# K and V loaded two heads at a time, on alternate partitions: a two-layer decode step on one Trainium2 core

## The chip, the core and the metric

The kernel runs on one core of one Trainium2 chip. A core has five engines that run their own instruction streams and meet at semaphores: TensorE (PE, with its weight loads shown apart as PEld), VectorE (DVE), ScalarE (ACT), GpSimd (POOL) and SyncE (SP), which here only issues DMAs. Data comes from HBM through 16 DMA engines into SBUF, which has 128 partitions; TensorE writes its products to PSUM, which has eight banks (here six tensors `bank0` to `bank5` and one tensor `pair` that holds the other two). The metric is the device time of one execution in microseconds (us).

## The reference

Eight batch rows of width 448 go through attention, an MLP, the same attention again and the same MLP again, each with a residual; layer norms have no weights.

```
x = x + A(layernorm(x));  x = x + B(layernorm(x));  x = x + A(layernorm(x));  x = x + B(layernorm(x))

A(x): q = (x @ wq) as [8 rows, 16 heads, 256]
      k, v = the last 1024 of 4096 positions of the caches [8 rows, 8 kv heads, 4096, 256]
      each kv head serves 2 of the 16 q heads
      o = softmax(q . k / 16) @ v;   return o (4096 wide) @ wo [4096, 448]
B(x): return silu(x @ w1 [448, 1792]) @ w2 [1792, 448]
```

Everything is bf16. Both layers use the same caches, so 64 pairs of a K head and a V head are read, each array 1024 x 256 x 2 bytes = 512 KB and contiguous in HBM; the next head of the same row begins 4096 x 256 x 2 bytes = 2 MiB further on. That is 67.1 MB of the 78.2 MB that the kernel moves.

## The kernel before

**Slots and loads.** A K or V head is one DMA of 512 KB (`load_kv`, L496): partition p gets eight consecutive positions, 4 KB in one piece. There are R = 30 slots of 4 KB per partition. The loads go round the slots in the order row 0 K heads 0 to 7, row 0 V heads 0 to 7, row 1 K, and so on (`seq`, `pump`), all on SP's queue, after `wq` (three loads with 8 KB per partition, L438), with `w2`, `wo` and `w1` in between. A load waits on SP until every reader of the load 30 places earlier is done. As a row takes 16 loads, V heads 6 and 7 of row b wait for K heads 0 and 1 of row b-1, K heads 0 to 5 of row b+1 for K heads 2 to 7 of row b-1, and K heads 6, 7 of row b+1 and V heads 0 to 5 of row b+1 for V heads 0 to 7 of row b-1. Whatever stands behind a waiting load on SP waits too.

**One row.** K is transposed in place by VectorE in blocks of 32 x 32 four-byte words (`transposes`, L639), four heads in one instruction each (128x1024 words) and four in two (128x512). `scores` (L656) multiplies block-diagonal queries (`qbd`) with the transposed K, four heads of a half k2 at a time on four column tiles of TensorE. `softmax` takes the maximum (L673), spreads it over groups of partitions (`mq` L674, matmul `mx` with `quad` L675, `mb` L677), takes the exponential (L688), permutes it with one matmul (`perm`, L690), transposes it on VectorE (`turn`, L692), sums it (`l`, L694) and inverts the sum (L697). `products` (L703) and `products_late` (L712, heads 6 and 7 of layer 1 and all of the last row's layer 2) multiply with V. `o_turn` (L725 to L733) turns the result, `wo_rows` (L754) multiplies with `wo`, `fold` (L760, L529, L532) adds the residual. `chain` is the MLP of layer 1 and the queries of layer 2: `stats` (L771 to L776), `w1_half` (L544, L549), tanh and product (`up`, L798 to L806), `w2` (L818), `wq` (L833, L838), `qm` and `qx` (L839, L846, L850).

**Order.** Row b's chain and its second attention (`attend2`, `values2`) are interleaved with the transposes, scores and products of row b+1 (`attend1`, `values1`); K and V of a row stay in their slots until layer 2 has read them. The order on PE, DVE, ACT and POOL is written out as task numbers in `ORDER`; each engine runs its list strictly in that order, and `Plan.emit` puts semaphore waits between tasks that share keys. The durations given with the tasks don't enter the program. SP's list is the program's order.

**The end.** The output projection and MLP of layer 2 are made for rows 0 to 6 together (`final_rows`, scratch in a slot of row 6), and for row 7 alone (`final_last`). `final_rows` begins with ten small VectorE instructions for the constants `fold8` and `f8a` (L874, L878, L880). In `up` for the last row, `th` (L801) multiplies with `rhalf` before `hT` (L803).

## Time and profile before

| | us |
|---|---|
| three timed runs: median (lowest to highest) | 231.98 (231.31 to 232.46) |
| the profiled execution: its own time | 230.15 |
| the profiled execution: its span, first to last instruction | 228.4 |
| busy: PE / DVE / ACT / POOL | 173.0 / 157.2 / 71.4 / 22.8 |

The granted TensorE clock is 1.00 throughout. The page divides the span into 40 slices of 5.7 us; a digit 9 is 90% busy or more. A group of instructions is told by its line, engine and operation, then written tile <- read tiles, shapes, count, busy time and the mean of one in ns. A matmul's duration is from its start to its modelled end, and matmuls overlap, so the time of a whole run of them in the chain or the timeline is the better price.

### The profile page before, as it was taken

To read this page: it belongs to the slowest core of one execution; us is meant where nothing else is said; L and a number is where in the kernel's file an instruction comes from. 1 tells how busy PE (TensorE), PEld (TensorE's weight loads), DVE (VectorE), ACT (ScalarE), POOL (GpSimd) and SP (SyncE) were. 2 spreads that over 40 slices of the span, in tenths; PEclk is the share of its full clock that TensorE was granted. 3 is DMA by queue.
4 is the path that set the end of the run, shared out by engine and by line. 5 is a ranking of instruction groups with operands and counts; after the bars stand their busy time and mean duration, and the time that the engine had idled before them with its cause. 6 is when DMAs were issued, how large, how long until landed. Compare 5 with 4: busy or idle time off the path is not lost.

```text
span 228.4 us, 8452 instructions
## 1 busy us (share of the span) xinstructions
PE 173.0 (76%) x3779; PEld 94.1 (41%) x3779; DVE 157.2 (69%) x369; ACT 71.4 (31%) x218; POOL 22.8 (10%) x41
## 2 busy tenths in 40 slices
PE   0020737357878989999898987888989999999894
PEld 0010623123444455445444644554445445544662
DVE  6238989878792797389459837974895589314644
ACT  2000080633302341432324142414332431353341
POOL 1000130000200210101010101110120200000020
PEclk9999999999999999999999999999999999999999
DMA  6999999999999999999999999999999999700000
GB/s 175 413 406 407 382 380 395 411 414 417 405 400 369 377 408 403 396 408 407 406 406 408 402 378 411 408 392 395 410 409 385 380 408 406 307 3 3 0 6 1
DMA packets 22681, 78.21 MB, mean 342 GB/s; under 512 B 2279, under 2 KB 5302, under 8 KB 22262
## 3 DMA queue, kind: packets, MB, share of 16 engines
q1 hardware_dynamic: 22486, 77.32, 86.6%
q8 instruction: 29, 0.48, 0.9%
q10 hardware_dynamic: 160, 0.36, 0.6%
q14 instruction: 6, 0.05, 0.1%
HBM read 77.67 MB, written 0.01 MB: 340 GB/s over the span
## 4 chain that ended last, share of the span: by engine, by line
PE 46%; DVE 31%; DMA 10%; ACT 6%; issue 4%; SPq 2%; DVEq 0%; ACTq 0%
DVE slot L639 12%; DMA slot<-in_A_k_cache_dram 10%; PE bank L656 10%; PE bank L703 7%; DVE slot L472 7%; PE pair L754 6%; PE bank L781 2%; PE pair L833 2%; ACT ot L760 2%; PE bank L675 2%; PE bank L846 2%; PE bank L712 2%; PE bank L833 2%; PE pair L529 2%; PE pair L818 1%
## 5 line engine op out<-in xcount | busy, mean ns | idle before, releaser
L639 DVE STREAM_TRANSPOSE slot<-slot 128x512 uint32<-128x512 uint32 (+1 forms) x96 | 80.2, 866 | 7.0 <-DMA slot<-in_A_k_cache_dram 6.8
L656 PE MATMUL bank<-slot,qbd 128*16 128x256 bf16 (+1 forms) x1024 | 40.9, 285 | 5.1 <-DVE slot L639 2.0
L703 PE MATMUL bank<-slot,qbd 128*24 128x512 bf16 (+6 forms) x416 | 31.1, 393 | 3.5 <-DVE qbd L692 3.3
L656 PEld LDWEIGHTS bank<-slot,qbd 128*16 128x16 bf16 (+1 forms) x1024 | 23.2, 87 | 16.7 <-ACT qbd L850 4.0
L781 PE MATMUL bank<-wq_sb,cols 128*1 128x512 bf16 x192 | 19.6, 416 | 13.9 <-DMA wq_sb<-in_A_wq_dram 13.9
L776 POOL TENSOR_TENSOR fcols<-fcols 128x1 f32<-128x1 f32 x17 | 9.4, 554 | 106.4 <-ACT fcols L774 94.5
L754 PE MATMUL pair<-wo_sb,q1s 128*1 128x449 bf16 x288 | 17.2, 353 | 1.1 <-DVE wo_sb L475 0.8
L850 ACT ACTIVATE qbd<-bank 128x256 bf16<-128x256 f32 x16 | 6.1, 384 | 33.5 <-PE bank L846 33.5
L725 ACT ACTIVATE ot<-bank,q1s 128x512 bf16<-128x512 f32 (+1 forms) x16 | 10.8, 673 | 16.4 <-PE bank L703 11.1
L626 POOL TENSOR_TENSOR qbd<-q1s,fcols 128x256 bf16<-128x256 bf16 x16 | 9.7, 614 | 59.7 <-PE bank L712 42.4
L703 PEld LDWEIGHTS bank<-slot,qbd 128*24 128x24 bf16 (+6 forms) x416 | 9.7, 92 | 11.1 <-DVE qbd L692 4.2
L692 DVE STREAM_TRANSPOSE qbd<-bank 128x256 bf16<-128x256 bf16 x17 | 8.0, 473 | 8.2 <-PE bank L690 7.9
L673 DVE TENSOR_REDUCE q1s<-bank 128x1 f32<-128x256 f32 x15 | 6.3, 423 | 8.1 <-PE bank L656 8.0
L472 DVE TENSOR_REDUCE slot<-wo_sb 128x6 f32<-128x2688 bf16 x4 | 11.8, 2948 | 0.1
L781 PEld LDWEIGHTS bank<-wq_sb,cols 128*1 128x1 bf16 x192 | 4.2, 82 | 15.4 <-issue 13.9
L674 ACT ACTIVATE q1s<-fcols,q1s 128x4 f32<-128x4 f32 x15 | 4.4, 296 | 18.7 <-DVE q1s L673 18.7
L675 PE MATMUL bank<-q1s,quad 128*128 128x4 f32 x30 | 6.0, 269 | 4.7 <-ACT q1s L674 4.5
L598 PE MATMUL pair<-slot,wq_sb 128*128 128x16 bf16 x128 | 3.6, 174 | 7.5 <-DVE slot L591 7.5
L833 PE MATMUL pair<-wq_sb,q1s 128*1 128x256 bf16 x256 | 8.9, 275 | 0.3 <-DVE q1s L765 0.3
L688 ACT ACTIVATE qbd<-bank,q1s 128x256 bf16<-128x256 f32 x15 | 7.1, 472 | 6.3 <-DVE q1s L677 6.0
L712 PE MATMUL bank<-slot,qbd 128*7 128x256 bf16 (+7 forms) x192 | 8.6, 283 | 0.6 <-DVE qbd L692 0.6
L833 PE MATMUL bank<-wq_sb,q1s 128*1 128x512 bf16 x128 | 8.8, 390 | 0.0
(168 smaller groups left out, 244.6 us busy)
## 6 DMA issues: line engine op xcount, KB each, us to landing
slot<-in_A_k_cache_dram SPq DMA_DIRECT2D x64, 512.0 KB, 8.3
slot<-in_A_v_cache_dram SPq DMA_DIRECT2D x64, 512.0 KB, 10.1
wo_sb<-in_A_wo_dram SPq DMA_DIRECT2D x4, 896.0 KB, 14.6
wq_sb<-in_A_wq_dram SPq DMA_DIRECT2D x3, 1024.0 KB, 8.0
w_sb<-in_B_w_dram SPq DMA_DIRECT2D x1, 1568.0 KB, 19.8
w_sb<-in_B_w_dram SPq DMA_DIRECT2D x1, 1344.0 KB, 17.2
wq_sb<-in_A_wq_dram ACTq DMA_DIRECT2D x1, 256.0 KB, 3.5
wq_sb<-in_A_wq_dram SPq DMA_DIRECT2D x1, 256.0 KB, 4.1
```

The source lines that it names most:

```text
L472: dve(lambda e, rows=rows, s=s: e.tensor_reduce(s, rows[:, :, R0:M1].rearrange("p c (a n) -> p c a n", a=2), AX.X, ALU.add, negate=True), ...
L626: pool(lambda e, k2=k2: e.tensor_tensor(qdata(0, k2), q1s[:, b, 64 * k2:64 * k2 + 64].rearrange("p (n r) -> p n r", r=2).unsqueeze(3) .bro ...
L639: dve(lambda e, v=v: e.transpose(v, v), keys, keys, 0.15 + n / 2 / 950, b, ("KW%d" if n > 1024 else "KT%d") % k)
L656: fns.append(lambda e, w=w, j=j, kv=kv, cb=cb, par=par: e.matmul(sc[32 * j:32 * j + up_to, 0:256], w, kv, start=(cb == 0 and par == 0), st ...
L675: pe(lambda e: e.matmul(mx, quad[:], mq, start=True, stop=True, skip_group_check=True), [K[4], "quad"], bk(LB[n]), 0.2, b, "mx%d" % L)
L703: pe([lambda e, t=t: e.matmul(bank[ob][32 * t:32 * t + m, :], pT_sb[L][:, 64 * t:64 * t + m], v[:, 512 * t:512 * t + 512], start=True, sto ...
L712: pe([lambda e, t=t, a=a: e.matmul(o[32 * t:32 * t + m, :], pT_sb[n][:, 64 * t + a:64 * t + a + m], v[:, 512 * t + DH * a:512 * t + DH * a ...
L725: act(lambda e: e.activation(o_t, src[1], ACTF.Copy, scale=sm[b][:, 4 * L + 3:4 * L + 4]), bk(src[0]) + [("sm", b, L, 3)], okey, 0.62, b, ...
L754: fns.append(lambda e, i=i, w=w, c0=c0: e.matmul(bank[XB][32 * (i % 4):32 * (i % 4) + 1, c0:c0 + D + 1], oT[:, oT_col(i):oT_col(i) + 1], w ...
L776: pool(lambda e: e.tensor_tensor(rhalf, var4, nhalf, ALU.pow), ["var4", "nhalf"], ["rhalf"], 0.54, b, "pow" + name)
L781: pe([lambda e, i=i: e.matmul(bank[OB[0]][32 * i:32 * i + 1, :], zero_b, wq_sb[:, 512 * i:512 * i + 512], start=True, stop=True, tile_posi ...
L833: pe([lambda e, j=j, c=c, qh=qh, k2=k2, h=h, n=n: e.matmul(qh[32 * j:32 * j + 1, :], xbt[b][:, xcol(c, k2):xcol(c, k2) + 1], view(wq_sb[:] ...
```

## The change

K and V heads are loaded in pairs. A slot is 8 KB per partition and there are 15 of them. Partition 2i + e of a pair gets sixteen consecutive positions of head e, 8 KB in one piece, so the two heads lie on alternate partitions. One DMA moves 1 MB. Only the very last pair (row 7, V heads 6 and 7) comes in two DMAs, each the first or second half of all rows, 4 KB per partition. The transposes now write each 32 x 32 block with the sixteen columns of the even partitions ahead of the sixteen of the odd ones, so that the scores' moving operand can pick a head. A product with V covers both heads of a pair: each `products` task is one half of a pair (the first or second 4 KB of each partition), with the other head's rows made zero. The softmax's permutation becomes four matmuls of 128 columns, with shifted views of two tables, and writes every other word; `mx` becomes four matmuls with 32-column weights; `mq` has 16 columns and one buffer. For the last row the factor `rhalf` moves behind the `w2` product, with the residual evicted apart by ScalarE (`resL`). The constants `fold8` and `f8a` are made behind row 1's second attention (`fold_consts`). The orders of the four engines are new.

```diff
-    R = 30
-    WIDE = (0, 1, 2, 3)
+    R = 15
+    NP = HKV // 2
+    WIDE = (0, 1)
+    SLOT = 4096
...
-    def load_kv(s, cache, b, kvh):
+    def load_kv(s, cache, b, j, apart):
         extra = SCRATCH[s] if s in SCRATCH and s not in first_use else []
         first_use.add(s)
-        dma(lambda e: e.dma_start(slots[s][:, :].rearrange("p (u d) -> p u d", d=DH),
-                                  cache[b, kvh, S0:SK, :].rearrange("(p u) d -> p u d", p=P)),
-            slot_key(s) + extra, W * DH * 2, "slot%d" % s)
+        a = cache[b, 2 * j, S0:SK, :]
+        step = SLOT // 2 if apart else SLOT
+        for h in range(SLOT // step):
+            src = bass.AP(a.tensor, a.offset + h * step, [[SLOT, 64], [SK * DH, 2], [1, step]])
+            dma(lambda e, h=h, src=src: e.dma_start(slots[s][:, h * step:(h + 1) * step], src),
+                slot_key(s, h if apart else None) + extra, P * step * 2, "last%d" % h if apart else "slot%d" % s,
+                rate=407e3 if apart else 417.7e3)
...
-    def transposes(b, k):
-        s = slot_of[b, "k", k]
-        n = 2048 if k in WIDE else 1024
-        for h in range(2048 // n):
-            v = slots[s][:, h * n:(h + 1) * n].bitcast(U32)
-            keys = slot_key(s) if n > 1024 else [("slot", s, h)]
-            dve(lambda e, v=v: e.transpose(v, v), keys, keys, 0.15 + n / 2 / 950, b,
-                ("KW%d" if n > 1024 else "KT%d") % k)
+    def transposes(b, j):
+
+        s = slot_of[b, "k", j]
+        for h in range(2):
+            for i0, i1 in ((0, 2),) if j in WIDE else ((0, 1), (1, 2)):
+                v = slots[s][:, 2048 * h + 1024 * i0:2048 * h + 1024 * i1].bitcast(U32)
+                keys = [("slot", s, 2 * h + i) for i in range(i0, i1)]
+                dve(lambda e, v=v, i0=i0, i1=i1: e.transpose(view(v, 0, [(32, 16 * (i1 - i0)), (1, 16), (16, 2)]), v), keys, keys,
+                    0.15 + (i1 - i0) * 512 / 950, b, ("KW%d" if i1 - i0 > 1 else "KT%d") % (2 * j + h))
...
-                    kv = slots[slot_of[b, "k", 4 * k2 + j]][:, :].rearrange(
-                        "p (u cb jj par) -> p cb par u jj", u=8, cb=4, par=2)[:, cb, par, :, :]
+                    kv = view(slots[slot_of[b, "k", 2 * k2 + j // 2]][:, :], 64 * cb + 32 * (j % 2) + par, [(256, 16), (2, 16)])
...
-            act(lambda e: e.activation(mq, sel4, ACTF.Copy, scale=mneg), [K[0], "sel4"], [K[4]], 0.2, b, "mq%d" % L)
-            pe(lambda e: e.matmul(mx, quad[:], mq, start=True, stop=True, skip_group_check=True), [K[4], "quad"],
-               bk(LB[n]), 0.2, b, "mx%d" % L)
+            act(lambda e: e.activation(mq, sel16, ACTF.Copy, scale=mneg), [K[0], "sel16"], ["mq"], 0.2, b, "mq%d" % L)
+            pe([lambda e, t=t: e.matmul(mx[32 * t:32 * t + 32, :], quad[:], mq[:, 4 * t:4 * t + 4], start=True, stop=True,
+                                        tile_position=(0, 32 * t), skip_group_check=True) for t in range(4)],
+               ["mq", "quad"], bk(LB[n]), 0.06, b, "mx%d" % L)
...
-        pe(lambda e: e.matmul(px, perm[:], e_sb[m], start=True, stop=True),
+        pe([lambda e, h=h, u=u: e.matmul(px[:, h:256:2], perm[h][:, 16 - 16 * u:144 - 16 * u],
+                                         e_sb[m][:, 128 * u:128 * u + 128], start=(u == 0), stop=(u == 1),
+                                         skip_group_check=True) for h in range(2) for u in range(2)],
            EK[m] + PERM + QM * m, bk(LB[n]), 0.13, b, "perm%d" % L)
...
-    def products(b, L, kvh, ob):
-        v = slots[slot_of[b, "v", kvh]]
-        m = 4 * (HKV - kvh)
-        pe([lambda e, t=t: e.matmul(bank[ob][32 * t:32 * t + m, :], pT_sb[L][:, 64 * t:64 * t + m],
-                                    v[:, 512 * t:512 * t + 512], start=True, stop=True, tile_position=(0, 32 * t),
-                                    skip_group_check=True) for t in range(4)],
-           slot_key(slot_of[b, "v", kvh]) + PT[L], bk(ob), 0.055, b, "PV%d" % L)
+    def products(b, L, j, ob):
+        v = slots[slot_of[b, "v", j]]
+        m = 8 * (NP - j)
+        for h in range(2):
+            pe([lambda e, t=t, h=h: e.matmul(
+                bank[ob][32 * t:32 * t + m, :], pT_sb[L][:, 64 * t + 32 * h:64 * t + 32 * h + m],
+                v[:, 2048 * h + 512 * t:2048 * h + 512 * t + 512], start=(h == 0), stop=(h == 1),
+                tile_position=(0, 32 * t), skip_group_check=True) for t in range(4)],
+               slot_key(slot_of[b, "v", j], h) + PT[L], bk(ob), 0.055, b, "PV%d" % L)
...
-            if name == "L":
-                dve(lambda e, t=t: e.tensor_scalar(t, t, 1.0, rhalf, op0=ALU.add, op1=ALU.mult), [("th", h), "rhalf"],
-                    [("th", h)], 0.12, b, "th" + n)
...
+    def fold_consts(n, row):
+        SM0 = [("sm", 0, L, i) for L in range(2) for i in range(5)]
+        for x in range(4):
+            dve(lambda e, x=x: e.tensor_copy(fold8[32 * x:32 * x + 32, :], ident[32 * x:32 * x + 32, 32 * x:32 * x + n]),
+                ["ident"], [("fold8", x)] + SM0, 0.08, row, "f8a")
+        for a in range(2):
+            dve(lambda e, a=a: e.tensor_copy(f8a[a], fold8), FOLD8 + SM0, [("f8a", a)], 0.08, row, "f8a")
+            for x in (1 - a, 3 - a):
+                dve(lambda e, a=a, x=x: e.memset(f8a[a][32 * x:32 * x + 32, :], 0.0), [("f8a", a)],
+                    [("f8b", a, x)], 0.08, row, "f8a")
...
-        dve(lambda e: e.tensor_copy(orow, ob[:, 0:T]), bk(OB[1]) + KEY, ["orowL"], 0.18, b, "orowL")
+        dve(lambda e: e.scalar_tensor_tensor(out=orow, in0=ob[:, 0:T], scalar=rhalf, in1=res, op0=ALU.mult, op1=ALU.add),
+            bk(OB[1]) + ["rhalf", "resL"] + KEY, ["orowL"], 0.2, b, "orowL")
...
-    seq = [(b, t, k) for b in range(NB) for t in "kv" for k in range(8)]
+    seq = [(b, t, k) for b in range(NB) for t in "kv" for k in range(NP)]
...
-    cap = [R - 2]
+    cap = [R - 1]
...
-        for kvh in range(HKV - LATE):
-            products(b, 0, kvh, OB[0])
+        for j in range(NP - 1):
+            products(b, 0, j, OB[0])
...
+        if b == 1:
+            fold_consts(NBF, 2)
```

## The prediction, written before the result was known

> **What bounds the kernel now.** I read the slices first, then the DMA rate by windows, then who waits for whom on SP and VectorE, then the groups by form, then the timeline of VectorE at the start and at the end. The slices of the page:

> ```profile
> DMA  6999999999999999999999999999999999700000
> GB/s 175 413 406 407 382 380 395 411 414 417 405 400 369 377 408 403 396 408 407 406 406 408 402 378 411 408 392 395 410 409 385 380 408 406 307 3 3 0 6 1
> ```

> The DMA engines are full from slice 2 to slice 34, that is to about 199 us, and then nothing is left to load: 28 us of computing on the last row follow. So the end is the end of the loads plus a tail. The loads run at 380 to 417 GB/s. The windows (start:end, length, then PE, PEld, DVE, ACT, POOL, clock, DMA share, GB/s) show what the rate depends on:

> ```profile
> 8.00:12.00 4.00, 0.00 (x0) 0.00 (x0) 0.00 (x0) 0.00 (x0) 0.00 (x0) 1.00 1.01 422
> 40.00:44.00 4.00, 1.54 (x10) 0.60 (x10) 3.30 (x7) 2.18 (x9) 0.00 (x0) 1.00 1.03 410
> 60.00:64.00 4.00, 3.41 (x81) 1.76 (x79) 2.89 (x7) 1.00 (x3) 0.55 (x1) 1.00 1.03 410
> 68.00:72.00 4.00, 3.24 (x74) 1.64 (x67) 1.09 (x5) 1.25 (x4) 0.00 (x0) 1.00 1.00 358
> 172.00:176.00 4.00, 3.56 (x87) 2.18 (x80) 1.79 (x5) 1.13 (x4) 0.00 (x0) 1.00 1.01 379
> ```

> From 8 to 12 us `wq` arrives in pieces of 8 KB: 422 GB/s. From 40 and from 60 V and K arrive in pieces of 4 KB: 410. The trace's packet records say the same: 4096 bytes take 160 ns (median; mean 165.5), 8192 bytes 314 (median). The dips to 358 and 379 fall behind moments when SP had been held by a slot. The waits, of SP and of VectorE (total, times, longest):

> ```profile
> SPq L496 <- PE bank L656: 59.5, 12, 8.9
> SPq L496 <- PE bank L703: 26.6, 18, 4.0
> DVE slot L639 <- DMA slot<-in_A_k_cache_dram: 6.8, 9, 1.8
> ```

> SP waits long, yet the DMA engines stay full, because loads are queued. Counting bytes issued less bytes landed, the queue is lowest when the second scores release K heads 0 and 1: 0.7 to 1.1 MB at 66.9, 88.7, 108.6, 130.1, 151.6, 172.6 and 193.1 us. That is 1.8 us of cover at 410 GB/s, and the period is 21.0 us per row. VectorE in turn waits for K, 5.6 of the 6.8 us between 60 and 161 us, and not once after 161. So loads and computing run in step, loads slightly ahead as the bound until 161 us.

> The instructions that the change touches (groups by form):

> ```profile
> L639 DVE STREAM_TRANSPOSE slot<-slot 128x512 uint32<-128x512 uint32 x64 | 41.2, 683 | 0.7 <-DMA slot<-in_A_k_cache_dram 0.7
> L639 DVE STREAM_TRANSPOSE slot<-slot 128x1024 uint32<-128x1024 uint32 x32 | 39.2, 1234 | 6.3 <-DMA slot<-in_A_k_cache_dram 6.1
> L692 DVE STREAM_TRANSPOSE qbd<-bank 128x256 bf16<-128x256 bf16 x17 | 8.0, 473 | 8.2 <-PE bank L690 7.9
> L690 PE MATMUL bank<-qbd,perm 128*128 128x256 bf16 x17 | 4.9, 289 | 3.1 <-ACT qbd L688 2.9
> ```

> **The change, part by part.**

> *Loads in 8 KB pieces.* 67.1 MB at 410 GB/s are 163.7 us, at 422 159.0: 4.7 us less. By the medians (2 x 160 against 314 ns) it is 1.9%, 3.1 us; by the mean of all 4 KB packets (331 against 314) 5.2%, 8.5 us, which would also cure the dips. The 422 was measured while no engine worked, so I stay between the first two: 4.0 us. Of the bytes, 39 of 187 us' worth come after 161 us, when nobody waited for them, so 79% pass on: **-3.2 us** (0 to -8.5). SP issues 65 loads in place of 128; an issue is 0.43 us against 1.28 us of transfer and never was the limit.

> *Pairs as the unit.* The first head of a pair is usable 1.28 us later (512 KB at 410). A load now waits for both heads of the pair it replaces, and all later loads stand behind it on SP, but K heads are already released four at a time by the scores, so only releases by V products get coarser. At the start the first transpose (15.8 us) moves to about 17.1; VectorE then has 0.6 us of waits for K and small idle gaps to give: **+0.3 us** (0 to 1.3). In steady state the lateness comes off the 1.8 us of cover, at nothing; without the cover it is 1.28 us in each of six rows (rival 3).

> *Transposes.* Same count and shapes, but the output alternates between two places 64 bytes apart. L692 also writes in a permuted pattern (steps of 4 bytes): 473 ns for 256 columns, against 445 for the plain one of L549 on 256 columns. Timeline of VectorE at the start:

> ```profile
> 6.03 0.35 DVE L403 TENSOR_REDUCE slot<-ident 128x32 f32<-128x128 bf16 x1
> 7.23 0.29 DVE L407 TENSOR_REDUCE slot<-ident 128x32 f32<-128x128 bf16 x1
> 29.36 1.28 DVE L604 TENSOR_TENSOR slot<-slot 128x256 bf16<-128x256 f32 x1
> ```

> L407 reads 128 elements in a row, L403 the same 128 in steps of 64 bytes: 0.06 us more, about 0.5 ns each. L604 writes 256 two-byte results in steps of 64 bytes and takes 1.28 us, where L591 (40 elements, 0.193) and L566 (8, 0.16) lead to 0.42: 3.4 ns more for each. I take **0**, from L692, because it is the nearest in kind (the same operation, with an output that is permuted inside a block), and because here each 16 bytes are filled within eight successive writes; the ends are 0 (the count of columns is the same, so no gain) and 3.4 ns per column over 65,536 columns, rival 1. [...]

> *Softmax.* `perm`: one matmul (0.28 us) becomes four of 128 columns; four of 64 columns (L846) span 0.42 in the chain, so about 0.53, +0.25 us. `mx`: two passes with 128-column weights (0.39) become eight with 32-column weights; the eight of L694 span 0.24, -0.15 us. In all +0.1 us in each of 15 softmaxes; in steady state TensorE's work lies beside loads that set the pace (cover as above; uncovered 1.5 us in all). In the tail one `perm` of row 7's layer 2 and the last layer 1 softmax are on the path: **+0.4 us**. Products and scores keep their number and columns; weights of 32 in place of 28 columns cost 399 against 396 ns: nothing.

> *The tail.* In row 7 the constants sit between steps of the chain:

> ```profile
> 204.98 0.47 DVE L549 STREAM_TRANSPOSE pair<-pair 128x256 f32<-128x256 f32 x1 [0.90 <-PE pair L544]
> 205.47 0.16 DVE L874 COPY slot<-ident 32x7 bf16<-32x7 bf16 x1
> 205.60 0.40 DVE L549 STREAM_TRANSPOSE bank<-bank 128x192 f32<-128x192 f32 x1
> 206.03 0.17 DVE L874 COPY slot<-ident 32x7 bf16<-32x7 bf16 x1
> 206.23 0.16 DVE L806 SCALAR_TENSOR_TENSOR q1s<-q1s,pair 128x8 bf16<-128x8 f32 x1
> ```

> From the first transpose to L806 it is 1.25 us here, 0.83 in the row before (164.98 to 165.81): -0.4. At 209.73 to 210.97 (L838 to L839) the memsets of L880 cost another 0.4 (1.24 against 0.84). Leaving out `th` (L801) saves 0.2 at 224.4. Together **-1.0 us**. The ten small instructions go to row 1, 1.2 us in a period in which VectorE idles 6 of 21 us. `resL` runs on ScalarE while TensorE does `w2`. The two half loads of the last pair are as long as the two heads they replace: 0.

> *Sum.* -3.2 + 0.3 + 0 + 0.4 - 1.0 = -3.5 us. The profiled execution took 230.15 us (span 228.4 and 1.75 around it); it would take 226.65. The median of the timed runs is 1.83 above the profiled one, 231.98, so I forecast 231.98 - 3.5 = **228.5 us**.

> **The rivals.**
> 1. *The transposes pay for the scattered write (slower).* For: L604 and L403. [...] At 0.5 ns per column (L403) VectorE gets 33 us more; of its transposes 28.5 us are in the chain that ended last (12.5% of the span), some 24,000 columns, so +12 us: about 240. At 3.4 ns it is 223 us, VectorE alone is busy 380 us, and the time about 400. It decides from 0.15 ns per column on, where 24,000 columns eat the 3.5 us.
> 2. *Computing sets the pace already (no change).* For: no wait for a load after 161 us, and the chain from there to the end holds none. Against: 5.6 us of waits for K before, and 1.8 us of queue at every release. The faster loads then give nothing, and the tail's -0.6 remains: 231.4.
> 3. *The queue runs dry.* Faster loads take 0.5 us per row off the queue, pairs up to 1.28 us, perm and mx 0.2; 1.8 is the cover. Where it is gone, the gain of the loads is eaten (231.4), and each of six rows is up to 1.28 us longer (239.1). As 2.0 us stand against 1.8, it would be nearer the lower end: 233.5.
> 4. *The two streams of a load, 2 MiB apart, read more slowly.* The slowest window, 358 GB/s, over 67.1 MB is 187 us against 164: +23, 251. No load of the trace has this source pattern. Against: within each head the pieces are contiguous, as `wq`'s are. [...]

> **How the numbers follow.** Forecast 65%, rival 1 12%, rival 2 10%, rival 3 9%, rival 4 4%. The forecast's own range is 225 (the loads at -5.7, the tail -1.0, the rest nothing: 225.3) to 231. The three runs spread by 0.5%, so 0.5% (1.2 us) is about what a measurement can tell from no change. Faster: nearly all of the forecast and little of rival 2, 0.65. Same: rival 2 and the upper edge of the forecast, 0.10. Slower: rivals 1, 3 and 4, 0.25. For 8 in 10 the range takes the forecast, rival 2 and the lower half of rival 3: 224.5 to 235.

> **What would show it.** Right: GB/s of 415 or more in the slices from 13 us on, the last load landed by about 196 us, a tail of 28 us or less after it, L639's two forms still near 683 and 1234 ns, the four perms spanning near 0.5 us and mx near 0.24. Wrong: means of L639 above 750 and 1370 ns (rival 1); rates as hoped but SP held longer and DMA digits below 9 (rivals 2 and 3); 8 KB packets far above 314 ns (rival 4).

## The result and the profile after

| | before | changed |
|---|---|---|
| timed runs: median (lowest to highest), us | 231.88 (231.31 to 232.46) | 262.92 (262.02 to 264.57) |
| the profiled execution: its own time, us | 230.15 | 262.02 |
| its span, us | 228.4 | 260.2 |
| busy PE / DVE, us | 173.0 / 157.2 | 177.5 / 192.5 |

The changed kernel is slower by a ratio of 1.135 (95% interval 1.128 to 1.141). It was forecast at 228.5 us. Ratios, here and below, leave out executions more than 1.5% above the fastest of the same kernel; medians and ranges take all of them.

The first place to look is the groups that the change touches. Transposes of K and score products, forms kept apart, in the changed kernel:

```profile
L653 DVE STREAM_TRANSPOSE slot<-slot 128x512 uint32<-128x512 uint32 x64 | 61.6, 1052 | 0.6 <-DMA slot<-in_A_k_cache_dram 0.5
L653 DVE STREAM_TRANSPOSE slot<-slot 128x1024 uint32<-128x1024 uint32 x32 | 59.4, 1916 | 9.9 <-DMA slot<-in_A_k_cache_dram 9.8
L669 PE MATMUL bank<-slot,qbd 128*16 128x256 bf16 x512 | 23.2, 293 | 7.3 <-DVE slot L653 4.6 <-ACT qbd L862 2.5
L669 PE MATMUL bank<-slot,qbd 128*8 128x256 bf16 x512 | 19.4, 293 | 9.0 <-DVE slot L653 9.0
```

Counts and shapes are those of before, but one transpose takes 1052 ns in place of 683, and 1916 in place of 1234. That is 369 ns more for 512 columns and 682 for 1024, 0.67 to 0.72 ns for each column, over 65,536 columns. The sums of these groups were 41.2 and 39.2 us before, so these groups are 40.6 us longer. VectorE's busy time as a whole rises by 35.3 us, as instructions that follow each other overlap at their ends (64 of 1052 ns would be 67.3 us; the group is busy for 61.6). The score products themselves are nearly as fast as before (293 against 285 ns, with a granted clock of 0.972 in this execution against 1.00); what is new is their wait for the transposes, 13.6 us for L653, against 2.0 us for L639 before.

The slices and the chain that ended last, from the page of the changed kernel:

```profile
DMA  6999999999489935995899599859993998410000
GB/s 189 417 426 393 380 400 419 421 424 418 166 329 429 397 145 219 419 419 241 336 419 422 215 424 422 351 181 348 419 334 103 423 421 369 133 39 3 3 5 1
...
DVE 53%; PE 22%; DMA 15%; ACT 4%; issue 3%; SPq 2%; DVEq 0%; ACTq 0%
DVE slot L653 37%; DMA slot<-in_A_k_cache_dram 15%; DVE slot L480 5%; PE bank L669 4%; PE bank L719 4%; PE bank L703 3%; DVE pair L850 2%; PE pair L772 2%; DVE bank L850 1%; DVE qbd L851 1%; PE bank L799 1%; ACT slot L488 1%; DVE pair L562 1%; PE pair L845 1%; DVE q1s L818 1%
```

Before, the DMA digits were 9 from slice 2 to slice 34. Now the traffic falls once in every row (166, 145, 241, 215, 181, 103 GB/s in a slice). The transposes, 12% of the chain before, are 37% of it, some 96 us. The windows show that the loads are not slow but absent (start:end, length, busy time of PE, PEld, DVE, ACT, POOL, clock, DMA share, GB/s):

```profile
108.00:112.00 4.00, 3.32 (x61) 1.41 (x57) 4.00 (x6) 0.86 (x4) 0.90 (x2) 1.00 1.01 426
120.00:124.00 4.00, 2.98 (x76) 1.98 (x72) 3.93 (x7) 0.77 (x2) 0.00 (x0) 1.00 0.18 72
96.00:100.00 4.00, 3.26 (x79) 1.98 (x75) 3.96 (x7) 0.77 (x2) 0.00 (x0) 1.00 0.00 0
```

While a load runs it moves 426 GB/s. Where the traffic stops, VectorE is busy without a gap (3.93 and 3.96 of 4 us): it is behind, the slots are not released, and the queue of loads runs empty. The longest of SP's waits say what it stood at (total, times, longest):

```profile
SPq L509 <- PE bank L669: 61.4, 10, 13.7
```

The score products release the slots, as before (59.5 us in 12 waits, the longest 8.9), but they stand behind the transposes now. All of SP's waits at a load of K or V add up to some 162 us; before, to some 106.

Each row now lasts 24.7 us in place of 20.3: softmax's exponentials come in pairs, one for each layer, and between the second of the first pair and the second of the seventh lie six rows, from 79.5 to 227.5 us, before from 74.8 to 196.5.

### The profile page after: what moved, and what is told of

It is laid out like the page before. It is cut to its first block, busy times and chain, and to the rows that moved or that the text cites. A ratio compares the mean times of both kernels' runs of the same rounds, so it can differ in the third digit from the quotient of the medians.

```text
span 260.2 us, 8680 instructions
## 1 busy us (share of the span) xinstructions
PE 177.5 (68%) x3920; PEld 100.7 (39%) x3920; DVE 192.5 (74%) x369; ACT 71.2 (27%) x219; POOL 22.8 (9%) x41
## 4 chain that ended last, share of the span: by engine, by line
DVE 53%; PE 22%; DMA 15%; ACT 4%; issue 3%; SPq 2%; DVEq 0%; ACTq 0%
DVE slot L653 37%; DMA slot<-in_A_k_cache_dram 15%; DVE slot L480 5%; PE bank L669 4%; PE bank L719 4%; PE bank L703 3%; DVE pair L850 2%; PE pair L772 2%; DVE bank L850 1%; DVE qbd L851 1%; PE bank L799 1%; ACT slot L488 1%; DVE pair L562 1%; PE pair L845 1%; DVE q1s L818 1%
## 5 line engine op out<-in xcount | busy, mean ns | idle before, releaser
L653 DVE STREAM_TRANSPOSE slot<-slot 128x512 uint32<-128x512 uint32 (+1 forms) x96 | 120.4, 1340 | 10.5 <-DMA slot<-in_A_k_cache_dram 10.4
L669 PE MATMUL bank<-slot,qbd 128*16 128x256 bf16 (+1 forms) x1024 | 41.0, 293 | 16.3 <-DVE slot L653 13.6
L669 PEld LDWEIGHTS bank<-slot,qbd 128*16 128x16 bf16 (+1 forms) x1024 | 24.8, 90 | 27.4 <-DVE slot L653 17.8
L719 PE MATMUL bank<-slot,qbd 128*24 128x512 bf16 (+3 forms) x416 | 29.8, 380 | 0.2 <-DVE qbd L707 0.2
L743 ACT ACTIVATE ot<-bank,q1s 128x512 bf16<-128x512 f32 (+1 forms) x16 | 10.8, 672 | 25.7 <-PE bank L719 19.2
L639 POOL TENSOR_TENSOR qbd<-q1s,fcols 128x256 bf16<-128x256 bf16 x16 | 9.7, 614 | 87.2 <-PE bank L747 42.7
L703 PE MATMUL bank<-qbd,perms 128*128 128x128 bf16 x68 | 11.0, 322 | 4.3 <-ACT qbd L701 4.3
L686 ACT ACTIVATE fcols<-fcols,q1s 128x16 f32<-128x16 f32 x15 | 4.6, 309 | 32.9 <-DVE q1s L685 31.3
L719 PEld LDWEIGHTS bank<-slot,qbd 128*24 128x24 bf16 (+3 forms) x416 | 9.7, 91 | 8.7 <-issue 1.9
L830 PE MATMUL pair<-w_sb,q1s 128*1 128x449 bf16 x112 | 8.3, 380 | 4.4 <-DVE q1s L818 4.3
L789 PE MATMUL bank<-q1s 128*128 128x1 bf16 x68 | 4.3, 167 | 10.2 <-DVE q1s L783 10.2
L712 DVE RECIPROCAL q1s<-bank 128x1 f32<-128x1 f32 x17 | 2.6, 162 | 11.7 <-PE bank L709 11.6
L488 ACT ACTIVATE slot<-w_sb 128x448 bf16<-128x448 bf16 x6 | 3.5, 576 | 23.7 <-DMA w_sb<-in_B_w_dram 23.6
```

The source lines that it names most:

```text
L639: pool(lambda e, k2=k2: e.tensor_tensor(qdata(0, k2), q1s[:, b, 64 * k2:64 * k2 + 64].rearrange("p (n r) -> p n r", r=2).unsqueeze(3) .bro ...
L653: dve(lambda e, v=v, i0=i0, i1=i1: e.transpose(view(v, 0, [(32, 16 * (i1 - i0)), (1, 16), (16, 2)]), v), keys, keys, 0.15 + (i1 - i0) * 51 ...
L669: fns.append(lambda e, w=w, j=j, kv=kv, cb=cb, par=par: e.matmul(sc[32 * j:32 * j + up_to, 0:256], w, kv, start=(cb == 0 and par == 0), st ...
L703: pe([lambda e, h=h, u=u: e.matmul(px[:, h:256:2], perm[h][:, 16 - 16 * u:144 - 16 * u], e_sb[m][:, 128 * u:128 * u + 128], start=(u == 0) ...
L719: pe([lambda e, t=t, h=h: e.matmul(bank[ob][32 * t:32 * t + m, :], pT_sb[L][:, 64 * t + 32 * h:64 * t + 32 * h + m], v[:, 2048 * h + 512 * ...
L743: act(lambda e: e.activation(o_t, src[1], ACTF.Copy, scale=sm[b][:, 4 * L + 3:4 * L + 4]), bk(src[0]) + [("sm", b, L, 3)], okey, 0.62, b, ...
```

## The experiments

The theory after the result: the transposes pay for writing alternately at two places 64 bytes apart (rival 1 of the prediction), and everything else in the forecast stands. The rivals were that the price comes of something else (contention with the transfers, the pairs, the orders), or that it can only be moved, not avoided.

**The write made plain, the read moved out of step.**

```diff
-                dve(lambda e, v=v, i0=i0, i1=i1: e.transpose(view(v, 0, [(32, 16 * (i1 - i0)), (1, 16), (16, 2)]), v), keys, keys,
+                dve(lambda e, v=v: e.transpose(v, v), keys, keys,
...
-                    kv = view(slots[...][:, :], 64 * cb + 32 * (j % 2) + par, [(256, 16), (2, 16)])
+                    kv = view(slots[...][:, :], 64 * cb + 2 * (j % 2) + par, [(256, 16), (4, 16)])
```

> The changed kernel, but VectorE transposes K in place in plain order, and the scores pick a head by reading the transposed K in steps of 8 bytes instead of 4. Everything else (pairs, 8 KB pieces, softmax, tail, orders) is the changed kernel's. Theory (the scattered output of the transposes is the whole loss): the two forms of the transposes go back to about 683 and 1234 ns, VectorE's busy time from 192 to about 155 us, no DMA digit under 9 before the last slices, the scores stay at about 41 us, and the time is 226 to 231 us, under the kernel before. Rival A (pairs as the unit drain the queue, or the new orders are bad): the transposes go back, but the time stays above 240 us. Rival B (TensorE pays for steps of 8 bytes): the scores' runs get longer by a third or more, time 232 to 245 us.

Measured: 254.9 us (254.38 to 256.39), ratio 1.103 (1.100 to 1.107). The transposes are back at their old times, and most of the loss stays. The scores show rival B's mechanism, but the time lies above its 232 to 245 us. In this kernel, by form:

```profile
L653 DVE STREAM_TRANSPOSE slot<-slot 128x512 uint32<-128x512 uint32 x64 | 41.3, 684 | 1.3 <-DMA slot<-in_A_k_cache_dram 1.2
L653 DVE STREAM_TRANSPOSE slot<-slot 128x1024 uint32<-128x1024 uint32 x32 | 38.6, 1227 | 9.6 <-DMA slot<-in_A_k_cache_dram 9.5
L669 PE MATMUL bank<-slot,qbd 128*16 128x256 bf16 x512 | 36.1, 405 | 5.1 <-ACT qbd L862 2.5 <-POOL qbd L639 2.1 <-DVE slot L653 0.5
L669 PE MATMUL bank<-slot,qbd 128*8 128x256 bf16 x512 | 32.1, 410 | 3.1 <-DVE slot L653 3.1
```

The score products now take 405 to 410 ns in place of 293, and their group 68 us in place of 43. So the interleaving of two heads is paid for once, on whichever engine undoes it: on VectorE by the write, or on TensorE by reading every fourth element.

**The scattered write alone, in the kernel before.** Only the output pattern of the transposes is changed there; K's positions then lie in another order than V's, so that softmax weights meet the wrong rows of V.

```diff
-            dve(lambda e, v=v: e.transpose(v, v), keys, keys, 0.15 + n / 2 / 950, b,
+            dve(lambda e, v=v, n=n: e.transpose(view(v, 0, [(32, n // 64), (1, 16), (16, 2)]), v), keys, keys, 0.15 + n / 2 / 950, b,
```

> The kernel before with one edit: the transposes write each block with its even columns ahead of its odd ones, as the changed kernel does. The scores read as before, so the positions of K stand in another order than V's rows: the weights of the products meet other rows of V. All work and its amount are as before. Theory: 1050 and 1900 ns per transpose, VectorE busy 157 + 40 = 197 us, DMA engines idle once a row, and a time of 255 to 268 us, the changed kernel's. Rival A (pairs or orders are the cause): the transposes may cost more, but the time stays under 240 us, since VectorE had 6 us of idle time in each row.

Measured: 263.77 us (263.07 to 265.37), ratio 1.142 (1.137 to 1.147), with the transposes at 1054 and 1905 ns and at 38% of the chain. One output pattern, without pairs, larger pieces, new softmax or new order, takes the kernel before to the time of the changed kernel, as the theory had it.

**What the patterns cost by themselves.** A program with nothing but one load of K, three transposes of 512 columns for each output pattern, and copies; no matmul, no transfer beside them.

```diff
+    forms = [("plain",    transpose to [(1, 512)]),
+             ("halves64", transpose to [(32, 16), (1, 16), (16, 2)]),            # the change's pattern
+             ("pairs64",  transpose to [(32, 16), (2, 8), (16, 2), (1, 2)]),     # two words side by side
+             ("quads64",  transpose to [(32, 16), (4, 4), (16, 2), (1, 4)]),
+             ("step8",  ... [(2, 512)]), ("step16", ... [(4, 512)]), ("step64", ... [(16, 512)]),
+             ("copy", ...), ("copy64", written alternately), ("read64", read alternately)]
```

> Only VectorE instructions over 512 four-byte columns, three of each form, no other work beside them; nothing of the model is computed. Forms in order: transposes written plain, alternating word by word between two places 64 bytes apart (the change), by two words, by four words, then in steps of 8, 16 and 64 bytes; then copies: plain, written alternating, read alternating. Theory (a line of 16 bytes wants a second write directly after the first): plain, two words, four words and steps of 8 bytes cost 0.65 to 0.7 us, the alternating one about 1.05, steps of 16 and 64 bytes as much or more. Rival C (any permuted output costs the transposer): two and four words also cost about 1.05. Rival D (the price comes from DMA writes or other engines in SBUF at the same time): the alternating form costs 0.7 us here. From the copies: 64-byte reads about 0.5 ns per element more, as L403 against L407 in the kernel before.

The groups (lines 29 to 35 are the seven transposes in the order above):

```profile
L34 DVE STREAM_TRANSPOSE step<-words 128x512 uint32<-128x512 uint32 x3 | 2.8, 1040 | 0.0
L30 DVE STREAM_TRANSPOSE halves<-words 128x512 uint32<-128x512 uint32 x3 | 2.7, 997 | 0.0
L35 DVE STREAM_TRANSPOSE step<-words 128x512 uint32<-128x512 uint32 x3 | 2.7, 993 | 0.0
L29 DVE STREAM_TRANSPOSE plain<-words 128x512 uint32<-128x512 uint32 x3 | 1.9, 683 | 3.6 <-DMA words<-in_A_k_cache_dram 3.6
L33 DVE STREAM_TRANSPOSE step<-words 128x512 uint32<-128x512 uint32 x3 | 1.9, 671 | 0.0
L31 DVE STREAM_TRANSPOSE pairs<-words 128x512 uint32<-128x512 uint32 x3 | 1.8, 668 | 0.0
L37 DVE COPY copy<-words 128x512 uint32<-128x512 uint32 x3 | 1.5, 613 | 0.0
L38 DVE COPY read<-words 128x512 uint32<-128x512 uint32 x3 | 1.1, 444 | 0.0
L36 DVE COPY copy<-words 128x512 uint32<-128x512 uint32 x3 | 1.0, 394 | 0.0
```

The price is there with no other engine at work: 997 ns against 683, that is 314 of the 369 ns that the kernel pays (where the other 55 come from was not looked for). It has two levels only, 668 to 683 ns and 993 to 1040. Steps of 8 bytes (L33, 671 ns) and two neighbouring words at a time (L31, 668) cost nothing; steps of 16 bytes (L34, 1040), of 64 bytes (L35, 993) and the alternating pattern (L30, 997) all cost about the same. In these rows the patterns that put two words in succession into each 16 bytes are free, and those that put one there at a time pay 310 to 357 ns for 512 columns. A copy pays 219 ns for writing alternately (L37 against L36) and only 50 ns for reading so (L38), 0.1 ns for each column, where 0.5 was expected from L403 against L407.

**Smaller pieces in the kernel with the plain write.** Every pair comes as two loads of 512 KB, with 4 KB per partition.

```diff
-            load_kv(slot_of[x], A_k_cache if x[1] == "k" else A_v_cache, x[0], x[2],
-                    x == (LAST, "v", NP - 1))
+            load_kv(slot_of[x], A_k_cache if x[1] == "k" else A_v_cache, x[0], x[2], True)
```

> As e1, but every pair comes in two loads of 512 KB, first and second half of both heads, in pieces of 4 KB, with the same order of all engines. Theory (the gain of the loads is the piece of 8 KB): the rate in full windows falls from 420 or more to about 410 GB/s, and the time is 2 to 5 us above e1's, 229 to 234 us. Rival E (loads do not bound e1): within 1 us of e1, or faster by up to 1 us, since halves arrive 1.3 us earlier.

Measured: 255.69 us (255.0 to 256.97), against 254.9. The difference of 0.8 us is less than the runs tell apart, and as rival E has it. TensorE is 65% of the chain of the kernel with the plain write (DMA 10%); there the size of the pieces makes no difference that shows.

**Both sides free.** To see the rest of the prediction without this price, both patterns are made cheap at once, at the cost of the result.

```diff
-                dve(lambda e, v=v, i0=i0, i1=i1: e.transpose(view(v, 0, [(32, 16 * (i1 - i0)), (1, 16), (16, 2)]), v), keys, keys,
+                dve(lambda e, v=v: e.transpose(v, v), keys, keys,
```

> The changed kernel with two things free at once: the transposes write plainly in place (as before, 684 and 1227 ns) and the score products read in steps of 4 bytes over 256 consecutive words (as before, 285 ns mean). Loads in 8 KB pieces, pairs, tables with zeros, the orders and the tail stay as in the changed kernel. The score products then read some words of the other head of the pair, so the output is not the reference's; no size, count or order of any instruction differs. Theory, that the whole loss is the layout's price (on VectorE when it writes alternate lines, on TensorE when it reads in steps of 8 bytes) and the rest of the prediction stands: 226 to 232 us, no row's end with the DMA engines idle for over 2 us. Rival F, that the pairs as a unit or the new orders cost by themselves: over 236 us, with the same gaps in the traffic at each row's end.

Measured: 235.58 us (235.4 to 237.69), against 231.79 (230.37 to 233.71) for the kernel before on that chip; ratio 1.015 (1.006 to 1.023). Transposes and scores have their old means (866 and 288 ns). So 27 of the 31 us lost are the pattern's. But what is left is not the gain of 3.5 us that was forecast; it is a loss of nearly 4. The page of this kernel (its profiled execution is the slowest of the five, 237.69 us, with a granted clock of 0.983):

```profile
DMA  6999999999999996998999999999977997500000
GB/s 167 407 422 413 379 380 417 413 428 421 418 382 421 418 406 268 428 418 332 385 425 420 379 427 421 388 350 418 392 293 279 421 421 311 185 0 6 0 6 1
...
PE 47%; DVE 20%; DMA 20%; ACT 7%; issue 2%; SPq 2%; DVEq 0%; ACTq 0%
```

The loads run at 413 to 428 GB/s where they don't stop, as forecast, yet they fall again between rows (268, 332, 293, 279), and the last of them come in the slice that begins at 200.5 us; before it was the one at 194.1.

**A whole kernel without the price: heads on pairs of partitions.** The patterns alone show the way (L31, 668 ns with two words at a time): if partitions 4g, 4g + 1 hold the first head and 4g + 2, 4g + 3 the second, the transpose can separate the heads two words at a time.

```diff
+                fns = [lambda e, r=r: e.dma_start(slots[s][r:P:4, :], bass.AP(
+                    a.tensor, a.offset + r // 2 * SK * DH + r % 2 * SLOT, [[2 * SLOT, 32], [1, SLOT]])) for r in range(4)]
...
-  e.transpose(view(v, 0, [(32, 16 * (i1 - i0)), (1, 16), (16, 2)]), v)
+  e.transpose(view(v, 0, [(32, 16 * (i1 - i0)), (2, 8), (16, 2), (1, 2)]), v)
```

> The changed kernel with K's heads on alternate pairs of partitions (0, 1 the first head, 2, 3 the second, and so on) in place of alternate partitions, and the transposes writing two words next to each other, then two in the other half of the 64 words. K's pair comes in four loads of 256 KB, one for each partition of a group of four, still in pieces of 8 KB; V, the products and everything else as in the changed kernel; the computation is whole. Theory, that the price is one for 16-byte lines that get one word only at a time, as the priced patterns alone showed: transposes 670 to 700 and 1220 to 1250 ns, and 226 to 234 us in all, within 3 us of the kernel with both sides free (more loads of a smaller size may cost up to 3 us). Rival G, that alternating between the halves has a price of its own inside this kernel, beside DMA and TensorE: transposes over 900 ns, 245 to 265 us.

Measured: 238.73 us (236.91 to 239.33), ratio 1.028 (1.019 to 1.036). The transposes of this kernel:

```profile
L657 DVE STREAM_TRANSPOSE slot<-slot 128x512 uint32<-128x512 uint32 x64 | 41.5, 686 | 1.9 <-DMA slot<-in_A_k_cache_dram 1.9
L657 DVE STREAM_TRANSPOSE slot<-slot 128x1024 uint32<-128x1024 uint32 x32 | 39.0, 1233 | 19.3 <-DMA slot<-in_A_k_cache_dram 18.9
```

It separates the heads at the old price and is 24 us faster than the changed kernel: these hung on one word against two. The time is above the theory's 226 to 234, as that of the kernel with both sides free is, and 3.2 us above the latter. Part of this may be the small loads: in the chain of this kernel SP's issues follow each other without a gap (start, length, what):

```profile
157.36 0.59 SPq L511
158.00 0.59 SPq L511
158.63 0.60 SPq L511
```

A load of 256 KB every 0.64 us is 410 GB/s, so with loads this small the issuing is as slow as the transfer; before, an issue took 0.43 us for 512 KB.

**Smaller pieces with both sides free** (the edit of the two halves, on this kernel).

```diff
+            load_kv(slot_of[x], A_k_cache if x[1] == "k" else A_v_cache, x[0], x[2], True)
```

> The kernel with both sides free, its pairs loaded as two halves of 512 KB in pieces of 4 KB instead of one MB in pieces of 8 KB (output as there, not the reference's). Theory, by the prediction's term for the larger pieces (3.2 us of loads): 2 to 4.5 us more than the kernel with both sides free. Rival H, that the pieces' size is not what moved the rate, or is hidden: within 1 us of it.

Measured: 241.63 us (240.74 to 243.42), 6.1 us more than with pieces of 8 KB; forecast 2 to 4.5. Here the loads do count, and by more than was forecast. SP has twice the issues, too, and SP is 20% of this kernel's chain that ended last, against 2%. The rate and the issues were not separated.

**What a strided read costs TensorE.** Score products alone, by the step of the moving operand.

```diff
+    steps = {"step2": [(1, 256)], "step4": [(2, 256)], "old4": [(256, 16), (2, 16)], "step8": [(4, 256)],
+             "new8": [(256, 16), (4, 16)], "step12": [(6, 256)], "step16": [(8, 256)], "step32": [(16, 256)],
+             "pairs8": [(4, 128), (1, 2)]}
```

> Nothing of the model is computed: after 24 products that keep TensorE busy, nine forms of the score product (16 weight columns, 256 moving columns of bf16, four tiles of 32 columns, 32 products of each form, twice round), the moving words read in steps of 2, 4, 8, 12, 16, 32 bytes, as runs of 16 in steps of 4 and of 8 bytes, and as pairs of 2-byte words every 8 bytes. No DMA and no VectorE work beside them. Theory, that TensorE pays for the step of 8 bytes by itself: forms in steps of 4 bytes 33 to 40 ns a product, of 8 bytes 55 to 65 ns, longer steps no less. Rival, that the price in the kernel came of meeting VectorE or DMA: steps of 8 bytes within 3 ns of those of 4.

The groups (lines 47 to 55 in the order above):

```profile
L47 PE MATMUL bank<-keys,weights 128*16 128x256 bf16 x64 | 2.1, 273 | 0.0
L49 PE MATMUL bank<-keys,weights 128*16 128x256 bf16 x64 | 2.3, 282 | 0.0
L51 PE MATMUL bank<-keys,weights 128*16 128x256 bf16 x64 | 4.1, 409 | 0.0
L52 PE MATMUL bank<-keys,weights 128*16 128x256 bf16 x64 | 5.9, 519 | 0.0
L53 PE MATMUL bank<-keys,weights 128*16 128x256 bf16 x64 | 7.7, 632 | 0.0
L54 PE MATMUL bank<-keys,weights 128*16 128x256 bf16 x64 | 7.8, 640 | 0.0
L55 PE MATMUL bank<-keys,weights 128*16 128x256 bf16 x64 | 2.3, 278 | 0.0
```

Divided by 64, a product occupies TensorE 33 to 36 ns with steps of 2 or 4 bytes, 64 with 8, 92 with 12 and 120 with 16 or 32. By these rows the price follows how many elements lie in 16 bytes: with four or more there is none, two cost double, one costs nearly four times. Two neighbours every 8 bytes (L55) are free again. At 1024 products, the 28 ns between L49 and L51 are 29 us of TensorE, and in the kernel with the plain write the group was 26 us longer than in the changed kernel (68.2 against 42.6 us). Two in succession, enough for VectorE's writes of four-byte words (L33 of the patterns, 671 ns against 683), are therefore not enough here: L51 has two elements in every 16 bytes and pays (64 ns a product against 36).

**The order.** Why is the kernel with both sides free not faster? First, its rows 0 to 7 were put in the old order, and the kernel before in the new one.

```diff
-    sel16, mq = fcols[:, 13:29], fcols[:, 29:45]
+    sel16, mqs = fcols[:, 13:21].bitcast(BF16), [fcols[:, 21 + 16 * i:37 + 16 * i] for i in range(2)]
```

(and the task numbers of `ORDER`, matched by row, name and occurrence)

> The kernel with both sides free (plain transposes, score products in steps of 4 bytes, output not the reference's), with rows 0 to 7 put back in the order that the kernel before had on each engine. For that order to be possible the column that softmax multiplies its maxima into needs a place for each of the two layers (the changed kernel has one for both, so the second layer's maxima of a row have to be multiplied before the next row's first); it gets two. Theory O, that what the free kernel still loses (235.6 against 231.8 us, where 228.5 was predicted) is the new order: 227 to 231 us. Rival U, that pairs as the unit of loading and the four products of softmax cost it: 234 to 238 us.

> The whole computation: K's heads on alternate pairs of partitions as two runs earlier, with the old order and the two places for the maxima. By theory O 229 to 234 us (238.7 with the new order); by rival U 236 to 240 us.

> The kernel before, with nothing changed but the order of rows 1 to 7 on each engine, which is the changed kernel's; the computation is whole. Theory O: 234 to 239 us, against 231.8. Rival U: 231 to 233 us.

Measured: both sides free with the old order 239.3 us (238.12 to 240.39), ratio 1.032 (1.025 to 1.040) against 1.015 with the new order; pairs of partitions with the old order 242.49 (239.41 to 244.9), ratio 1.036 (1.025 to 1.046) against 1.028 (1.019 to 1.036), which is not clear of the noise; the kernel before with the new order 239.09 (237.45 to 240.62), ratio 1.031 (1.022 to 1.041). Each theory fails on one kernel: the old order makes the free kernel slower, not faster, and the new order costs the kernel before 7 us, where rival U had nothing. An order fits the kernel that it was written for. The new one is worth about 4 us (1.7%) to the kernel with both sides free, so it isn't where the rest of the forecast went.

**One product in softmax.**

```diff
-        pe([lambda e, h=h, u=u: e.matmul(px[:, h:256:2], perm[h][:, 16 - 16 * u:144 - 16 * u], ...) for h in range(2) for u in range(2)],
+        pe(lambda e: e.matmul(px, perm[0][:, 16:144], e_sb[m], start=True, stop=True),
```

> The kernel with both sides free and the new order, with softmax's four products of 128 columns made one of 256 columns, as in the kernel before (the weights then lie in the wrong columns for the pairs: output not the reference's). It takes away 0.25 to 0.3 us a softmax, 17 times, from TensorE and from the chain. If TensorE's time in the rows sets the pace, 231 to 233 us (235.6 with four products); if the loads or the order do, 234.5 to 236 us.

Measured: 235.09 us (233.53 to 236.75), ratio 1.014 (1.004 to 1.024) against 1.015 with four products. The perms' group fell from 10.8 to 4.9 us on TensorE, and the time did not follow by more than the 0.5 us between the medians, well inside the spread. Nothing here shows that TensorE's time in the rows sets the pace.

**Half the loads, first try.** Every load after the first use of a slot brings partitions 0 to 63 alone, in three kernels.

```diff
+        part = P // 2 if s in first_use else P
...
+            dma(lambda e, h=h, src=src: e.dma_start(slots[s][0:part, h * step:(h + 1) * step], src),
```

> The kernel with both sides free and the new order, in which every load of K and V after the first use of a slot brings partitions 0 to 63 alone, still in pieces of 8 KB: half the bytes, the same loads, waits and products (the other partitions keep what an earlier load left, so the output is not the reference's). Theory C, that the row's own chain of computing sets its pace once the writes and reads are free, and not the loads: 233 to 236.5 us, as with whole loads (235.6). Rival L, that landing and freeing by pairs of one MB, so a coupling to the loads, costs what is lost: under 231 us.

> The kernel before with the same cut: loads after the first use of a slot bring partitions 0 to 63 alone (output not the reference's). It shows what the computing of the kernel before needs by itself. Theory C wants it well under 231.8 us, for the chain of waits of that kernel goes through a load in every row: 222 to 229 us. If it stays at 230 to 232 us, its computing was as long as its loads, and no faster load could have helped.

> The changed kernel with the same cut (output not the reference's). That VectorE's transposes set its pace and the gaps in its traffic follow from them: 259 to 263 us, as with whole loads (262.9). That VectorE's writes are slowed by the transfers beside them, or that it waits for loads: under 256 us, with transposes shorter than 1052 and 1916 ns.

Measured: 252.0 us (251.21 to 253.28) with both sides free, 242.32 (241.11 to 243.13) for the kernel before, 266.2 (264.34 to 267.63) for the changed one. All three are slower, which no theory had. The windows of the first show why:

```profile
120.00:124.00 4.00, 4.00 (x84) 2.01 (x81) 1.29 (x4) 0.76 (x3) 0.00 (x0) 1.00 0.98 197
128.00:132.00 4.00, 2.99 (x69) 1.39 (x66) 3.75 (x7) 2.00 (x5) 0.55 (x1) 1.00 1.06 213
```

The DMA engines are as busy as ever (0.98, 1.06) at half the rate. A packet of 8 KB takes 645 ns in place of 309. So half the bytes took the whole time, and the runs tell nothing of what faster loads would give; why the time rose by 10 and 16 us in the first two kernels, and not only stayed, is open. The changed kernel, at 266.2 us, is not under the 256 us that it was to take if transfers slowed its transposes, so these runs show no such price.

**Half the loads, on all partitions.**

```diff
+            src = bass.AP(a.tensor, a.offset + h * step, [[SLOT, 64], [SK * DH, 2], [1, step // cut]])
+            dma(lambda e, h=h, src=src: e.dma_start(slots[s][:, h * step:h * step + step // cut], src),
```

> The kernel with both sides free again, now with the first 4 KB of each 8 KB piece on all 128 partitions in every load after the first use of a slot (output not the reference's). With partitions 0 to 63 alone the traffic fell to about 205 GB/s, so that those loads took as long as whole ones and told nothing of what the computing needs; on all partitions the rate should be that of 4 KB pieces, about 408 GB/s in full stretches, so the loads take half the time. Theory C (the row's chain of computing sets the pace once writes and reads are free): 232 to 237 us. Rival L (landing and freeing by pairs, so a coupling to the loads, costs what is lost): under 231 us.

> The kernel before, with 2 KB in place of each piece of 4 KB on all partitions in every load after the first use of a slot (output not the reference's). Theory C, by which the kernel before waits for loads in its rows and its computing is shorter than theirs: 222 to 229 us. If its computing is as long as its loads: 230 to 232 us, and then no faster load could have made it faster.

Measured: 230.41 us (229.87 to 230.78) with both sides free, ratio 0.989 (0.984 to 0.995); 230.41 (229.11 to 231.97) for the kernel before, ratio 0.993 (0.988 to 0.997), against 232.77 (230.35 to 236.42) for the kernel before untouched on that chip. The slices and the chain of the first, then of the second:

```profile
GB/s 173 411 417 416 379 381 408 422 421 422 419 364 365 256 95 47 355 270 74 193 324 217 45 339 215 149 147 308 118 173 192 322 229 7 92 3 3 0 6 1
...
PE 53%; DVE 21%; DMA 11%; ACT 9%; issue 3%; SPq 3%; DVEq 0%; ACTq 0%
```

```profile
GB/s 174 409 406 409 381 379 398 407 417 413 407 378 211 201 272 88 253 242 241 153 286 191 116 218 268 252 59 248 275 161 132 241 233 141 94 3 3 0 6 1
...
PE 46%; DVE 33%; ACT 7%; DMA 6%; issue 3%; SPq 3%; DVEq 0%; ACTq 0%
```

From slice 13 on the loads now leave the DMA engines idle half of the time, and both kernels stop at the same 230.4 us: that is what the computing needs, in its order, as far as halved loads can show it. Behind the start, no load is in the chain of either: the last one ends at 31.5 us in the first (a load of `wo`) and at 21.8 in the second (K). The kernel before has only 0.7% (0.3 to 1.2) between this floor and its time, so faster loads could give it some 1.7 us (0.7 to 2.7), and part of that may be the granted clock, which was 0.96 to 0.98 in seven of the eleven executions that this ratio takes of it and 0.997 or more in nine of the ten with halved loads. The kernel with both sides free has 5.2 us above its floor, by the ratios to the kernel before 2.5%, 5.9 us. So it does lose to its loads, although they are faster, as rival L has it; and the computing of the kernel before is nearly as long as its time. Theory C falls on both sides.

The chain of the kernel with both sides free shows where (start, length, what), with VectorE's waits for K below:

```profile
90.30 10.03 DMA slot<-in_A_k_cache_dram
154.36 10.07 DMA slot<-in_A_k_cache_dram
178.34 10.13 DMA slot<-in_A_k_cache_dram
...
DVE slot L653 <- DMA slot<-in_A_k_cache_dram: 20.5, 10, 8.0
```

In three rows the chain goes from the score products that free the slots through a load of K to its transposes; before, it does so through one load in the rows (9.39 us from 115.54), and VectorE waits 6.8 us for K in all. From one row's exponential to the next, these three rows are 1.7, 2.5 and 2.7 us longer than with halved loads and the others equal, 7.0 us together, which is the whole difference of the two spans (235.9 and 228.9). Counted as in the prediction, bytes issued less bytes landed, the queue falls to 0.5, 0.0, 0.1, 0.5, 0.3 and 0.0 MB at the score products of the rows, in the kernel before to 0.6 to 1.0.

**The tail alone, in the kernel before.** The constants moved to rows 2 to 7, `th` left out, the residual read out by ScalarE.

```diff
+    def fold_consts(n, row):
...
+            dve(lambda e, t=t, y=y, o=o: e.scalar_tensor_tensor(out=o, in0=t, scalar=1.0, in1=y, op0=ALU.add,
+                                                                op1=ALU.mult), bk(i) + [("th", h)], [("hT", h)],
...
+        dve(lambda e: e.scalar_tensor_tensor(out=orow, in0=ob[:, 0:T], scalar=rhalf, in1=res, op0=ALU.mult, op1=ALU.add),
```

> The kernel before with nothing but the changed kernel's tail: the ten small selections made in rows 2 to 7 instead of at the end, the last row's two scalings taken out and put into the last instruction, the residual read out on ScalarE; whole computation. The prediction took 1.0 us off for it: 230.3 to 231.4 us on a chip where the kernel before takes 231.8. If the selections were hidden or come to lie in the way of the rows, 231.5 to 233 us.

Measured: 231.56 us (229.74 to 234.03, 12 runs), ratio 1.000 (0.996 to 1.004). Its profiled span is 227.9 us against 228.4. If the tail gives anything it is about the half microsecond of the trace, which the timed runs can't tell from nothing. No kernel that computes the whole came out faster than the kernel before.

## Why the prediction was wrong, step by step

**The step that failed: *Transposes*, taken as 0.** The working had a row for either answer, L604 (a write in steps of 64 bytes, 3.4 ns each) and L692 (a permuted write without a price), and chose L692 as the nearest in kind and because each 16 bytes are filled within eight writes; the second reason had no row of the trace behind it. What counted in the runs is whether 16 bytes get two words one after the other, not whether they are filled soon: L30 against L31 of the patterns alone, 997 against 668 ns for the same destinations in another grouping. That it is this write that costs the time, the kernel before shows, which the pattern alone takes to 263.77 us, and the pairs of partitions, which separate the heads without it. The measured price is 0.67 to 0.72 ns for each column, by the means, and 40.6 us of the groups. Rival 1 was worked out with 0.5, which is near, but by luck: L403 is a read, and the one scattered read that was run, alternating between two places, costs a copy 0.1 ns for each column, where writing so costs it 0.4. Why L604 pays 3.4 ns for an element is not shown.

**Rival 1's own time was too low.** It was given as about 240 us, from the 28.5 us of transposes that lay on the chain before: a share of the chain taken from a kernel in which VectorE was not behind. Once VectorE is behind, its transposes take 37% of the chain, some 96 us, and 31 of the 40.6 us come through. In that proportion, as an estimate, the 33 us of 0.5 ns would have been 25, and the rival 257 us in place of 240.

**Loads in 8 KB pieces, -3.2 us.** The rate was right: 413 to 428 GB/s in slices without a gap (forecast 422), 309 ns for a packet (314, by the medians). The far end of the range, -8.5 us, was worked out from a mean of the 4 KB packets against a median of the 8 KB ones; the mean of the latter in that trace is 331 ns, too, as much as two of the former. The worth was not right: with half the loads the kernel before still needs 230.4 us, so it had about 1.7 us to gain. Here the prediction's rival 2, computing sets the pace already, was right in substance at 231.4 us; it got 10%. The waits of VectorE for K, 5.6 us in the rows, were read as proof that the loads were the bound; with a floor 0.7% below the time they show only that two sides were nearly equal.

**Pairs as the unit, +0.3 us.** The lateness was to come off the cover in the queue, at nothing. With both sides free the kernel is 5 to 6 us above its own computing, and its queue runs down to between 0.0 and 0.5 MB between rows, as rival 3 had it (233.5 to 239.1 us; measured 235.6). The loss lies in three rows that wait for a load of K. Which of its causes empties the queue, faster loads, landing and freeing by pairs, or a moved release, was not separated; this stays open. The new orders, which the sum has no term for, are worth 4 us to this kernel and cost the kernel before 7.

**Softmax, +0.4 us.** The four perms span 0.60 to 0.61 us in the traces, but for the first ones (forecast 0.53), and the eight of `mx` 0.24 as forecast. Making one product of the four moved the time by -0.5 us, less than the runs tell apart, so they don't contradict the term and can't confirm it.

**The tail, -1.0 us.** -0.5 us between two profiled spans, 0.0 +/- 0.9 in the time: by the spans, about half of what was forecast. Of the 0.8 us expected between the last two pairs of exponentials 0.3 came (19.3 us before, 19.0 with the new tail), of the 0.2 behind them 0.2 (12.3 to 12.1).

**Rival 4, two streams 2 MiB apart.** Wrong, as thought: 420 and more GB/s with that source pattern.

## What to carry to other kernels

Before a layout is interleaved, look at the words that follow each other in one instruction on both sides of it: in these runs a VectorE write wanted two four-byte words in a row for each 16 bytes (668 to 683 ns for 512 columns, 993 to 1040 without them), a TensorE read four two-byte elements (33 to 36 ns a product, 64 to 120 with fewer), and a pattern that broke this cost much on either engine (41 us of VectorE's transposes, 26 us of TensorE's products). If interleaving is wanted, interleave in groups that keep to this; the transposes that separate the heads by pairs of words kept their old price (686 and 1233 ns). And where loads and computing are close in time, find the floor of the computing by halving the loads on all partitions before pricing faster ones: here the floor of the computing lay 0.7% below the time, which no view of the waits had shown.
